# Last output-projection group in four column tiles of one PSUM bank, with the rest added by an identity product and two half copies

## Chip, cores, metric

One core of a Trainium2 chip. The metric is device time in microseconds (us) of one execution; lower is better. Before: 664.06 us, median of 3 runs (663.97 to 664.31).

## The reference, cut to what matters

```python
xn = layernorm(x)                                   # x: 4 x 1 x 640, bf16
q  = (xn @ wq) -> 4 x 32 heads x 128
p  = softmax(q @ k_cache^T * 128**-0.5)             # k_cache, v_cache: 4 x 32 x 4096 x 128
A  = (p @ v_cache -> 4 x 4096) @ wo                 # wo: 4096 x 640
out = x + A + gated_mlp(xn)                         # out: 4 x 640, bf16
```

Two caches of 134 MB each make nearly all of the 282.6 MB that the kernel moves. The heads are worked in four groups of eight. The last group's share of `@ wo`, and the adding up of all shares, is the last thing that happens. In the code below, PSUM is the memory that TensorE writes its sums to, a PSUM tile is a named piece of it (`ps_l.tile` and `misc_ps` allot one), and a bank is the block of PSUM in which the tile lies. In a profile line, 128\*4 or 64\*64 gives the rows and columns of a product's weights.

## The kernel before

The feed-forward part and the wo shares of groups 0 to 2 add up in one PSUM tile, `proj`: even wo pieces c in rows 0 to 63, odd ones in rows 64 to 127; within 64 rows, columns 0 to 319 of the output lie in rows 0 to 3, columns 320 to 639 in rows 32 to 35. VectorE adds those two halves and the residual `x_res` into `o_1`. The last group's pieces go to two further PSUM tiles, and VectorE adds those to `o_1`. The last group's wo is loaded in four parts: c = 0 to 3, 4 and 5, 6, 7.

```python
NG, HG, NH, NO2, B = 4, 8, 2, 320, 4
...
load_wo(NG - 1, (0, 4, 6, 7, 8))
...
o_1 = ppool.tile([64, NO2], F32)
nc.vector.tensor_tensor(out=o_1, in0=proj[0:64, 0:NO2], in1=x_res, op=ALU.add)
nc.vector.tensor_tensor(out=o_1, in0=proj[64:128, 0:NO2], in1=o_1, op=ALU.add)
last_a = ps_l.tile([64, NO2], F32)
last_b = misc_ps([P, NO2], F32)
last = [last_a, last_b[64:128]]
part = {1: 1, 3: 1, 5: 1}                # c = 1, 3, 5 to last_b, the others to last_a
for c in range(HG):
    p = part.get(c, 0)
    ...                                  # 32 columns of weights in a tile's first product, then 4
    for hf in range(NH):
        nc.tensor.matmul(last[p][32 * hf:32 * hf + nb, :], lhsT=lhsT,
                         rhs=wo_t[NG - 1][:, c, hf * NO2:(hf + 1) * NO2], start=..., stop=...)
    if c == 5:
        nc.vector.tensor_tensor(out=o_1, in0=last[1], in1=o_1, op=ALU.add)
o_bf = ppool.tile([64, NO2], BF16)
nc.vector.tensor_tensor(out=o_bf, in0=last[0], in1=o_1, op=ALU.add)
nc.sync.dma_start(out=out_flat[:, 0:NO2], in_=o_bf[0:B, :])
nc.scalar.dma_start(out=out_flat[:, NO2:NOUT], in_=o_bf[32:32 + B, :])
```

## Time and profile before

| | before |
|---|---|
| device time, median | 664.06 us |
| span of the profiled run | 662.5 us |
| DMA, mean | 427 GB/s |
| first product of the last group to store issue | 657.42 to 660.00 = 2.58 us |
| first c = 4 product to store issue | 658.21 to 660.00 = 1.79 us |
| clock of TensorE from 656.2 us on | 0.50 |

The kernel streams from HBM until about 658.5 us. Of the profile's rows only the last three can be touched by this change; the lines behind them are in the prediction. I call the stretch from the first product of the last group to the issue of the first store **the tail** in what follows. It starts with a landing load, so it can be compared between runs whose loads land at slightly different times.

### The profile page before, as it was taken

The numbers are of one execution on the slowest core, as the hardware profiler recorded it, in microseconds if no ns is written. First come the engines' busy times: TensorE is split into PE (matmuls) and PEld (weight loads), VectorE is DVE, ScalarE is ACT, GpSimd is POOL, SyncE is SP. The second block draws the span as 40 slices with busy tenths as digits, with TensorE's granted clock in tenths as the row PEclk, the third lists the DMA queues.
The fourth block names the chain that finished last, engine by engine and source line by source line (L and its number), as shares of the span: only waits on it lengthen the run. The fifth ranks groups of instructions, "written<-read, shape, count | busy, mean of one in ns | idle before, by whom it ended". The sixth has DMA issues, their size and how long they took to land.

```text
span 662.5 us, 5421 instructions
## 1 busy us (share of the span) xinstructions
PE 292.9 (44%) x2297; PEld 106.5 (16%) x2297; DVE 360.1 (54%) x275; ACT 78.4 (12%) x162; POOL 20.3 (3%) x64
## 2 busy tenths in 40 slices
PE   0636666256072556225336054533506254623245
PEld 0111122112021122111112022111202112211122
DVE  2249899556191759618256286745619185951112
ACT  0300000530100000530200000071010000053200
POOL 6210000000000000000000000000000000000000
PEclk9858768678577587677859596756958759667767
DMA  9999999999999999999999999999999999999996
GB/s 371 463 424 427 426 444 437 435 436 416 443 432 423 439 418 442 433 439 440 423 420 435 432 421 452 433 424 431 431 436 444 428 431 415 445 432 437 418 419 262
DMA packets 6901, 282.61 MB, mean 427 GB/s; under 512 B 808, under 2 KB 1084, under 8 KB 1468
## 3 DMA queue, kind: packets, MB, share of 16 engines
q1 hardware_dynamic: 6856, 282.25, 98.8%
q8 instruction: 18, 0.29, 0.2%
q14 instruction: 7, 0.06, 0.0%
q10 hardware_dynamic: 20, 0.01, 0.0%
HBM read 282.25 MB, written 0.01 MB: 426 GB/s over the span
## 4 chain that ended last, share of the span: by engine, by line
DMA 74%; DVE 11%; issue 11%; PE 2%; ACT 1%; SPq 0%; DVEq 0%; ACTq 0%
DMA kv<-in_A_k_cache_dram 64%; DVE kT L367 11%; DMA kv<-in_A_v_cache_dram 5%; DMA kv<-in_A_wo_dram 3%; DMA kv<-in_A_wq_dram 2%; PE O L449 2%; ACT xd L432 0%; ACT Zb L413 0%; ACT p L421 0%; DVE pT L425 0%; PE last_a L553 0%; DVE m L385 0%; PE S L378 0%; SPq L169 0%; PE misc L390 0%
## 5 line engine op out<-in xcount | busy, mean ns | idle before, releaser
L367 DVE STREAM_TRANSPOSE kT<-kv 128x2048 f32<-128x2048 f32 x128 | 282.8, 2276 | 124.7 <-DMA kv<-in_A_k_cache_dram 124.7
L378 PE MATMUL S<-kT,QZ 128*32 128x512 bf16 x1024 | 187.9, 500 | 230.6 <-DVE kT L367 230.6
L378 PEld LDWEIGHTS <-QZ 128*32 128x32 bf16 x1024 | 60.3, 111 | 353.4 <-issue 332.6
L449 PE MATMUL O<-kv,Zb 128*32 128x512 bf16 x1024 | 73.6, 451 | 58.2 <-DMA kv<-in_A_v_cache_dram 38.0
L458 DVE TENSOR_TENSOR om<-O,Mk 128x512 f32<-128x512 f32 x15 | 10.4, 692 | 109.0 <-PE O L449 109.0
L413 ACT ACTIVATE Zb<-xd,MkE 32x256 bf16<-32x256 bf16 x116 | 52.9, 498 | 110.4 <-PE O L449 109.0
L421 ACT ACTIVATE p<-S,negmax 128x512 bf16<-128x512 f32 x8 | 5.4, 683 | 400.6 <-DVE negmax L399 400.6
L449 PEld LDWEIGHTS <-Zb 128*32 128x32 bf16 x1024 | 32.9, 112 | 97.4 <-issue 55.8
L472 PE MATMUL misc<-R,SelR 128*32 128x128 f32 x32 | 6.4, 281 | 30.0 <-DVE R L459 28.4
L353 POOL COPY QZ<-qT 32x32 bf16<-32x32 bf16 x16 | 5.1, 318 | 390.6 <-PE S L378 389.9
L432 DVE COPY xd<-pT 32x256 bf16<-32x256 bf16 x44 | 16.0, 365 | 0.8
L459 DVE TENSOR_REDUCE R<-om 128x128 f32<-128x512 f32 x15 | 15.3, 1019 | 0.5
L432 ACT COPY xd<-pT 32x256 bf16<-32x256 bf16 x20 | 12.3, 614 | 5.6 <-DVE pT L425 5.2
L425 DVE STREAM_TRANSPOSE pT<-p 128x1024 bf16<-128x1024 bf16 x4 | 5.0, 1245 | 6.3 <-ACT p L421 6.3
L472 PEld LDWEIGHTS misc<-R,SelR 128*32 128x32 f32 x32 | 2.2, 107 | 37.8 <-DVE R L459 26.0
L385 DVE TENSOR_REDUCE m<-S 128x2 f32<-128x1024 f32 x4 | 4.9, 1225 | 5.5 <-PE S L378 5.5
L274 PE MATMUL q<-kv,xnT 128*32 128x512 bf16 x40 | 4.5, 630 | 6.9 <-DMA kv<-in_A_wq_dram 6.9
L461 DVE TENSOR_SCALAR R<-O,Mk 128x128 f32<-128x128 f32 x1 | 0.4, 351 | 12.5 <-PE O L449 12.5
L282 DVE CAST kv<-q 128x512 bf16<-128x512 f32 x1 | 0.7, 692 | 11.1 <-PE q L274 11.1
L390 PE MATMUL misc<-dg,ones_f 128*128 128x256 f32 x8 | 3.2, 488 | 7.6 <-DVE dg L387 7.6
L475 DVE SCALAR_TENSOR_TENSOR om<-misc,rinv,SelH 32x1024 bf16<-32x1024 f32 x4 | 5.1, 1271 | 2.0 <-PE misc L472 2.0
L437 PE MATMUL misc<-rowsum,SelPe 128*32 128x1 f32 x16 | 2.1, 202 | 9.0 <-ACT p L421 9.0
(102 smaller groups left out, 78.2 us busy)
## 6 DMA issues: line engine op xcount, KB each, us to landing
kv<-in_A_k_cache_dram SPq DMA_DIRECT2D x8, 4096.0 KB
kv<-in_A_v_cache_dram SPq DMA_DIRECT2D x1, 6144.0 KB
kv<-in_A_wq_dram SPq DMA_DIRECT2D x1, 5120.0 KB
kv<-in_A_wo_dram SPq DMA_DIRECT2D x3, 1280.0 KB
kv<-in_B_w_in_dram SPq DMA_DIRECT2D x1, 2160.0 KB, 19.9
kv<-in_A_v_cache_dram SPq DMA_DIRECT2D x1, 2048.0 KB
kv<-in_B_w_out_dram SPq DMA_DIRECT2D x1, 800.0 KB
kv<-in_A_wo_dram SPq DMA_DIRECT2D x1, 640.0 KB, 22.0
```

The costliest lines, as they stand in the source:

```text
L353: nc.gpsimd.tensor_copy(out=QZ[r0:r0 + 32, :, :, :, 8 + 8 * hp], in_=qT[32 * g:32 * g + 32, NE * hp:NE * hp + NE].rearrange("p e a b -> p ...
L367: nc.vector.transpose(kT[:].rearrange("p (t r) -> p t r", r=32), kw)
L378: nc.tensor.matmul(S_ps[32 * q:32 * q + 32, e], lhsT=QZ[:, b, 2 * kh + w, e, w0:w0 + 32], rhs=kb[:, i, :, e, :, w], start=(b == 0 and k < ...
L413: nc.scalar.activation(out=dst, in_=src, func=ACT.Copy, scale=mk)
L421: nc.scalar.activation(out=p_bf[:, :, e, :], in_=S_ps[:, e], func=ACT.Exp, bias=negmax[:, e:e + 1], scale=scale, accum_out=rowsum[:, e:e + 1])
L425: nc.vector.transpose(pT[:].rearrange("p t h x -> p (t h x)"), p_bf[:].rearrange("p t e m -> p (t e m)"))
L432: op(out=xd[32 * hp:32 * hp + 32, :, q, :], in_=pT[32 * q:32 * q + 32, :, hp, :].rearrange("p t x -> p x t"))
L449: nc.tensor.matmul(O_ps[32 * q:32 * q + 32, :, :], lhsT=Zb[b % 2][:, w].rearrange("p h c -> p (h c)"), rhs=vv[:, w * 4 * Dh:(w + 1) * 4 * ...
L458: nc.vector.tensor_tensor(out=om4[:], in0=O_ps[:], in1=Mk4[:, :, None].to_broadcast((P, 4, Dh)), op=ALU.mult)
L459: nc.vector.tensor_reduce(out=R, in_=om4[:].rearrange("p c d -> p d c"), axis=AX.X, op=ALU.add)
L472: nc.tensor.matmul(oh[:], lhsT=SelR[:, b].rearrange("p h b -> p (h b)"), rhs=state["R"][:, b, :], start=(b == 0), stop=(b == B - 1))
L475: nc.vector.scalar_tensor_tensor(out=om[:], in0=oh[:, None, :].to_broadcast((G, HG, Dh)), scalar=state.pop(("rinv", g))[:, 0:1], in1=MkH[: ...
```

## The change

It is meant to shorten what follows the last landing. All four column tiles of 32 take part for every c, so each product has 160 columns instead of 320. `o_1` no longer has to be added by VectorE: TensorE adds it with an identity matrix as weights (`ident_f`, in FP32). Two engines then copy half the result each.

```diff
-    last_a = ps_l.tile([64, NO2], F32)
-    last_b = misc_ps([P, NO2], F32)
-    last = [last_a, last_b[64:128]]
+    NQ = NO2 // 2
+    last = ps_l.tile([P, NQ], F32)
     ...
     for c in range(HG):
-        for hf in range(NH):
-            nc.tensor.matmul(last[p][32 * hf:32 * hf + nb, :], lhsT=lhsT,
-                             rhs=wo_t[NG - 1][:, c, hf * NO2:(hf + 1) * NO2], ...)
-        if c == 5:
-            nc.vector.tensor_tensor(out=o_1[:], in0=last[1], in1=o_1[:], op=ALU.add)
+        for k in range(2):
+            for hf in range(NH):
+                r0, n0 = 64 * k + 32 * hf, hf * NO2 + k * NQ
+                nc.tensor.matmul(last[r0:r0 + nb, :], lhsT=lhsT, rhs=wo_t[NG - 1][:, c, n0:n0 + NQ],
+                                 start=c == 0, stop=c == HG - 1)
+        if c == HG - 4:
+            for k in range(2):
+                nc.tensor.matmul(last[64 * k:64 * k + 64, :], lhsT=ident_f[:64, :64], rhs=o_1[:, k * NQ:(k + 1) * NQ],
+                                 start=False, stop=False)
-    nc.vector.tensor_tensor(out=o_bf[:], in0=last[0][:], in1=o_1[:], op=ALU.add)
+    nc.vector.tensor_copy(out=o_bf[:, 0:NQ], in_=last[0:64, :])
+    nc.scalar.copy(out=o_bf[:, NQ:NO2], in_=last[64:128, :])
```

(A padding column of zeros that the first products of the old layout needed, and its memset, go.)

More of the change, by code (lines that the diff above doesn't have):

```diff
@@ L484, in emit_oT @@
             nc.tensor.matmul(oT_ps[:, c, :], lhsT=om[:, c, :, :], rhs=B32[:], start=True, stop=True)
-        oT = small.tile([P, HG + 1, B], BF16, tag="oT", bufs=3)
-        nc.vector.tensor_copy(out=oT[:, 0:HG, :], in_=oT_ps[:])
-        if g == NG - 1:
-            nc.gpsimd.memset(oT[:, HG, :], 0.0)
+        oT = small.tile([P, HG, B], BF16, tag="oT", bufs=3)
+        nc.vector.tensor_copy(out=oT[:], in_=oT_ps[:])
         state[("oT", g)] = oT
@@ L540 @@
     nc.vector.tensor_tensor(out=o_1[:], in0=proj[64:128, 0:NO2], in1=o_1[:], op=ALU.add)
-    last_a = ps_l.tile([64, NO2], F32)
-    last_b = misc_ps([P, NO2], F32)
-    last = [last_a, last_b[64:128]]
+    NQ = NO2 // 2
+    last = ps_l.tile([P, NQ], F32)
     oT = state[("oT", NG - 1)]
-    part = {1: 1, 3: 1, 5: 1}
-    seen = set()
     for c in range(HG):
-        p = part.get(c, 0)
-        lhsT = oT[:, c, :] if p in seen else oT[:, c:c + HG, :].rearrange("p c b -> p (c b)")
-        nb = B if p in seen else 32
-        for hf in range(NH):
-            nc.tensor.matmul(last[p][32 * hf:32 * hf + nb, :], lhsT=lhsT,
-                             rhs=wo_t[NG - 1][:, c, hf * NO2:(hf + 1) * NO2], start=p not in seen, stop=c in (5, HG - 1))
-        seen.add(p)
-        if c == 5:
-            nc.vector.tensor_tensor(out=o_1[:], in0=last[1], in1=o_1[:], op=ALU.add)
+        lhsT = oT[:, c:c + HG, :].rearrange("p c b -> p (c b)") if c == 0 else oT[:, c, :]
+        nb = 32 if c == 0 else B
+        for k in range(2):
[7 more added lines that the diff above has]
+                                 start=False, stop=False)
     o_bf = ppool.tile([64, NO2], BF16, tag="p", name="o_bf")
-    nc.vector.tensor_tensor(out=o_bf[:], in0=last[0][:], in1=o_1[:], op=ALU.add)
+    nc.vector.tensor_copy(out=o_bf[:, 0:NQ], in_=last[0:64, :])
+    nc.scalar.copy(out=o_bf[:, NQ:NO2], in_=last[64:128, :])
     nc.sync.dma_start(out=out_flat[:, 0:NO2], in_=o_bf[0:B, :])
```

## The prediction

> **What bounds the kernel now.** I read the page's slice table first, then the chain of waits at the end, the timeline of the last microseconds, short windows over the same stretch, and the groups by line and shape for durations.
>
> The page says that the kernel streams: 427 GB/s in the mean, DMA at 90% or more in 39 slices of 40.
>
> ```profile
> DMA  9999999999999999999999999999999999999996
> DMA packets 6901, 282.61 MB, mean 427 GB/s; under 512 B 808, under 2 KB 1084, under 8 KB 1468
> ```
>
> The change touches nothing before the last loads of wo, so 656 us of the 662.5 us span cannot move. What it can move is the tail: from the last loads to the end. The timeline of that tail, before:
>
> ```profile
> 655.89 1.01 PE L496 MATMUL proj<-kv,oT 128*4 128x320 bf16 x16 [1.09 <-DMA kv<-in_A_wo_dram]
> 656.94 0.48 DVE L539 TENSOR_TENSOR o<-proj,x_res 64x320 f32<-64x320 f32 x1 [1.91 <-PE proj L496]
> 657.42 0.45 PE L553 MATMUL last_a<-kv,oT 128*32 128x320 bf16 x2 [0.52 <-DMA kv<-in_A_wo_dram]
> 657.46 0.49 DVE L540 TENSOR_TENSOR o<-proj,o 64x320 f32<-64x320 f32 x1
> ...
> 658.21 0.43 PE L553 MATMUL last_a<-kv,oT 128*4 128x320 bf16 x2
> 658.22 0.43 PE L553 MATMUL misc<-kv,oT 128*4 128x320 bf16 x2
> 658.62 0.83 PE L553 MATMUL last_a<-kv,oT 128*4 128x320 bf16 x4
> 658.62 0.08 PEld L553 LDWEIGHTS <-oT 128*4 128x4 bf16 x2 [0.32 <-issue]
> 658.70 0.49 DVE L557 TENSOR_TENSOR o<-misc,o 64x320 f32<-64x320 f32 x1 [0.74 <-PE misc L553]
> 659.02 0.08 PEld L553 LDWEIGHTS <-oT 128*4 128x4 bf16 x1 [0.32 <-issue]
> 659.49 0.48 DVE L560 TENSOR_TENSOR o_bf<-last_a,o 64x320 bf16<-64x320 f32 x1 [0.30 <-PE last_a L553]
> 660.00 0.30 SPq L561 DMA_DIRECT2D out_dram<-o_bf  x1
> 660.01 0.27 ACTq L562 DMA_DIRECT2D out_dram<-o_bf  x1
> ```
>
> The last group's wo comes in four pieces: columns c = 0 to 3 (0.66 MB), 4 and 5 (0.33 MB), 6 (0.16 MB), 7 (0.16 MB). Products start at 655.89 (the group before, 0.66 MB last), 657.42, 658.21, 658.62 and 659.02, so 1.53, 0.79, 0.41 and 0.40 us apart. Bytes over those gaps are 428, 415, 400 and 410 GB/s: the kernel's DMA rate. I therefore read each piece as starting when its load lands, also c = 6 and 7, where the page names "issue" because records of earlier products overlap. Then the end is: last landing 659.02, one product of 0.43 us, one VectorE add of 0.48 us, then store issue at 660.00 and 2.5 us to the end of the span.
>
> One more thing sets the sizes, the granted clock (columns: window, PE, PEld, DVE, ACT, POOL, clock, DMA share, GB/s):
>
> ```profile
> 652.80:656.20 3.40, 1.67 (x36) 1.17 (x39) 1.46 (x2) 0.00 (x0) 0.00 (x0) 1.00 0.85 341
> 656.20:659.60 3.40, 2.67 (x29) 0.74 (x20) 1.58 (x4) 0.00 (x0) 0.00 (x0) 0.50 0.24 84
> ```
>
> The tail runs at half clock. The same 320-column product takes 299 ns (median, L496) at full clock and 427 ns (L553) here: 133 + 166 and 267 + 160 with 320 columns at 2.4 and 1.2 per ns. So a product is its columns over the clock plus about 165 ns.
>
> **What the Trainium skill says.** (1) "TensorE: Matmul & The Clock Gate", section "What's actually happening": the array gets half its clock after an idle window of about 3.4 us, in free-running windows. The trace agrees: 1.00 to 0.50 at 656.2, and 2.4 and 1.2 columns per ns fit both durations. (2) "FP8 and Floating Point Precision", section "TensorE Precision Notes": true FP32 is four passes through the array. The trace agrees: each FP32 product has two records, and one of 256 columns takes at least 379 ns at full clock, which is 2 x 256 / 2.4 + 166. (3) "TensorEngine Tiling (Array Packing)", section "Key Properties": changing the tiling mode drains TensorE. The trace of before shows no such change with nothing else between, so this is untested. (4) "PSUM — Partial Sum Buffer", section "PSUM bank collisions raise a hardware error": two engines may use one bank at once if they are in different quadrants. So the two halves could be copied out side by side; whether the program lets them is another matter (below).
>
> **Removed.** Two 64x320 adds: the one at 658.70 (0.49 us) ends at 659.19 and is off the path; the final one (0.48 us at 659.49) is on it. The 320-column products become 160 columns wide, each c filling all four column tiles. For the last c that is 320 - 160 columns, 133 ns less at half clock (0.43 to 0.29 us). A GpSimd memset at 429 us goes, worth nothing.
>
> **Added 1: the identity products.** After c = 4 come two FP32 products of 64 rows, 64 weights and 160 columns. At half clock one record is two passes of 160: 2 x 160 / 1.2 = 267 ns of streaming, and there are four records, two per half. If the two halves ran fully side by side: 0.53 us. In order with the second record of one beside the first of the other: three steps, 0.80 us. Strictly one after another: 1.07 us. They also change the tile from 128x32 to 64x64 and back; if that drains the array, about 0.16 us each way (the fixed part of a product). Their input is ready in time: the second add ends at 657.95, and c = 4 lands at 658.21.
>
> Walk it with the middle choice and drains. c = 4 starts at 658.21, is through at 658.21 + 0.13 + 0.17 = 658.51. Identity streams to 659.31 and drains to 659.47. c = 5, 6 and 7, now all landed, take 3 x 0.133 us, and the last result is there at 659.47 + 0.40 + 0.16 = 660.03. Before it was 659.45: **plus 0.58 us**. Fully side by side and without drains: 658.35 + 0.53 + 0.40 + 0.16 = 659.44, no loss, no gain. Strictly in series with drains: plus 0.85 us. The slack between the landing of c = 4 and that of c = 7 is 0.81 us; c = 4 to 6 fill 0.40 us of it, so about 0.4 us of identity is free and the rest pushes the end.
>
> **Added 2: the two copies.** VectorE casts from PSUM: 128x32 in 192 ns and 128x512 in 692 ns, so 159 ns + 1.04 ns an element, and 64x160 is 0.33 us. ScalarE from PSUM: 320 elements in 437 ns and 512 in 586 ns, so 189 + 0.78 an element: 0.31 us. Side by side they would take 0.33 instead of 0.48 us, a gain of 0.15 us. But the listing of the built program's instruction order with the semaphores that each waits for shows the ScalarE copy waiting on VectorE's counter alone, not on TensorE's, and both stores waiting on ScalarE. VectorE's only late instruction is its own copy: the copies run **one after the other**. That is 0.33 + about 0.05 hand-over + 0.31 = 0.69 us for 0.48 us: **plus 0.21 us**.
>
> The sum of the middle case is +0.58 + 0.21 = +0.79 us. I take less than that as my point, because of the cases below.
>
> **Rivals.** *The change works as meant*: identity hidden in the load waits and copies side by side: -0.13 - 0.15 = -0.28 us, 663.8 us. For it: the input of the identity is early and 0.81 us of load time lies open. Against it: the half clock, and the semaphore listing, which is not an estimate. *Full clock in the tail*: windows run free, so unprofiled runs may meet the tail at full clock. Identity then streams in 0.40 us, c = 5 to 7 take 0.07 us each, and the walk ends at 658.21 + 0.23 + 0.40 + 0.17 + 0.20 + 0.16 = 659.37 against 659.02 + 0.30 = 659.32: plus 0.05, with the copies plus 0.26 us, 664.3 us. In the profiled run the clock fell exactly at 656.2, so this is the less likely one. *TensorE becomes the bound of the tail in full*: series and drains, +0.85 + 0.21 = +1.06 us, 665.1 us. *The copies alone count* (halves concurrent, no drains): +0.21 us, also 664.3 us. Nothing here reaches the loads: same sizes, same order, same waits.
>
> **Range and chances.** Weights by my reading: middle case 0.45 (664.85), copies alone or full clock 0.35 (664.3), series 0.15 (665.1), as meant 0.05 (663.8). The mean is 0.45 x 0.79 + 0.35 x 0.24 + 0.15 x 1.06 - 0.05 x 0.28 = +0.58 us, so 664.06 + 0.58 = 664.64; I say **664.6 us**. The runs of before spread over 0.34 us, a chip may differ as much, so the range is **664.1 to 665.2 us**. Two per cent is 13.3 us, more than the whole stretch from the landing of c = 4 to the end (4.3 us): within 2% at 0.99, faster and slower 0.005 each.
>
> **What would show it.** In the timeline after: c = 7's products no longer start at a fixed 0.40 us after c = 6's but follow it at 0.13 us, behind four FP32 records that span some 0.8 us (right), or c = 7 still starts near 659.0 with TensorE idle ahead of it (wrong: identity was hidden). The ScalarE copy starts after the VectorE copy's end and is released by it (right), or beside it (wrong). Copies of 0.33 and 0.31 us; store issue near 660.8 instead of 660.00. Loads landing at the same times, DMA near 427 GB/s. A time under 664.0 us would mean that the serial copies or the FP32 passes cost less than their shapes say; over 665.3 us, that the switch of tile mode costs far more than a drain.

## The result, and the profile after

The changed kernel took 664.62 us (median of 5; 664.49 to 665.95), the kernel before 664.31 us in all its 5 runs (663.97 to 665.42). The ratio is 1.0004, 95% interval 0.9992 to 1.0017. A ratio here is the mean time of one kernel's fast runs over that of the other's of the same rounds, so not quite the ratio of the medians quoted.

The interval is about 0.8 us either way, wider than the effect, because single runs of either kernel reach 665.4 and 665.9 us while most lie below 665. So single terms are read below from the traces, one for each version, and the medians are put beside them.

The timeline of the changed kernel's tail (start, duration, engine, line, operation; the idle time before it and its releaser in brackets):

```profile
657.48 1.09 PE L548 MATMUL last<-kv,oT 128*32 128x160 bf16 x20 [0.29 <-DMA kv<-in_A_wo_dram]
657.76 0.49 DVE L538 TENSOR_TENSOR o<-proj,o 64x320 f32<-64x320 f32 x1
658.27 0.09 PEld L548 LDWEIGHTS <-oT 128*4 128x4 bf16 x3 [0.30 <-issue]
658.50 0.80 PE L552 MATMUL last<-o,ident_f 64*64 64x160 f32 x4
659.23 0.57 PE L548 MATMUL last<-kv,oT 128*4 128x160 bf16 x12
659.85 0.32 DVE L556 CAST o_bf<-last 64x160 bf16<-64x160 f32 x1 [1.60 <-PE last L548]
660.20 0.29 ACT L557 CAST o_bf<-last 64x160 bf16<-64x160 f32 x1 [40.10 <-DVE o_bf L556]
660.52 0.30 SPq L558 DMA_DIRECT2D out_dram<-o_bf  x1
660.52 0.27 ACTq L559 DMA_DIRECT2D out_dram<-o_bf  x1
```

Two things are to be seen. First, c = 4 lands at 658.27 (the first weight load that had waited with it), the identity products run from 658.50, and the twelve products of c = 5, 6 and 7 follow in one block at 659.23, with no gap of 0.4 us between them any more: TensorE is late for c = 6 and 7, which have already landed (at 658.64 and 659.04 by the landing records). Their last result is there at 659.80, 1.53 us after c = 4's landing, where it was 659.45 - 658.21 = 1.24 us before: 0.29 us more. Second, ScalarE's copy names VectorE's as its releaser and starts when that has ended. From the last product to the store it is 0.72 us instead of 0.55: 0.17 us more.

The tail is 660.52 - 657.48 = 3.04 us instead of 2.58: **0.46 us more**. The span grew by 0.4, the median time by 0.31 us. From the store to the end of the span it is 2.41 us instead of 2.47, so 0.06 us of the tail's growth is given back there.

### The profile page after: what moved, and what is told of

Same layout as the page of the kernel before. It is cut to its first block, busy times and chain, and to the rows that moved or that the text cites. A ratio compares the mean times of both kernels' runs of the same rounds, so it can differ in the third digit from the quotient of the medians.

```text
span 662.9 us, 5457 instructions
## 1 busy us (share of the span) xinstructions
PE 292.8 (44%) x2317; PEld 106.8 (16%) x2317; DVE 359.8 (54%) x274; ACT 78.7 (12%) x163; POOL 20.2 (3%) x63
## 4 chain that ended last, share of the span: by engine, by line
DMA 74%; DVE 12%; issue 10%; PE 2%; ACT 1%; SPq 0%; DVEq 0%; ACTq 0%
DMA kv<-in_A_k_cache_dram 64%; DVE kT L367 11%; DMA kv<-in_A_v_cache_dram 5%; DMA kv<-in_A_wo_dram 3%; DMA kv<-in_A_wq_dram 2%; PE O L449 2%; ACT xd L432 0%; PE S L378 0%; ACT Zb L413 0%; ACT p L421 0%; DVE pT L425 0%; DVE m L385 0%; PE misc L390 0%; PE last L548 0%; SPq L169 0%
```

## The experiments

All ten runs were compared with runs of the kernel before on the same chip. All gave right results except the one that was not meant to. In the table, tail is the stretch defined above, read from each run's timeline; the median of before is that of the same call.

| kernel | tail, us | tail against before | median, us | before, us | ratio (95% interval) |
|---|---|---|---|---|---|
| before | 2.58 | | | | |
| the change | 3.04 | +0.46 | 664.62 | 664.31 | 1.0004 (0.9992 to 1.0017) |
| e1_two_banks | 2.73 | +0.15 | 664.29 | 664.33 | 1.0002 (0.9990 to 1.0014) |
| e2_early | 2.97 | +0.39 | 664.67 | 664.33 | 1.0005 (0.9993 to 1.0017) |
| e3_both | 2.64 | +0.06 | 664.51 | 664.33 | 1.0002 (0.9990 to 1.0014) |
| e4_one_sum | 2.34 | -0.24 | 664.00 | 664.33 | 0.9997 (0.9984 to 1.0010) |
| e5_same_half (wrong result) | 3.57 | +0.99 | 665.11 | 664.25 | 1.0013 (0.9998 to 1.0028) |
| e6_same_mode | 2.75 | +0.17 | 664.27 | 664.25 | 1.0001 (0.9984 to 1.0018) |
| e7_warm_before | 2.45 | -0.13 | 663.96 | 664.25 | 0.9996 (0.9981 to 1.0011) |
| e8_warm_after | 2.57 | -0.01 | 664.04 | 664.25 | 0.9997 (0.9982 to 1.0012) |
| e9_one_sum_warm | 2.27 | -0.31 | 664.11 | 664.29 | 0.9997 (0.9982 to 1.0011) |
| e10_mode_banks | 2.45 | -0.13 | 664.14 | 664.29 | 0.9997 (0.9985 to 1.0009) |

**The theory:** the loss is two separate terms, TensorE's time for the identity beyond what the load waits hide, and the two copies in series. **The rivals:** the copies could not run side by side anyway; the identity was hidden and something else moved the end; the half clock alone made the loss.

### Two banks

```diff
-    last = ps_l.tile([P, NQ], F32)
+    last_a = ps_l.tile([64, NQ], F32)
+    last_b = misc_ps([P, NQ], F32)
+    last = [last_a, last_b[64:128]]
```

(The products and copies now name `last[0]` or `last[1]`.)

> Only the two halves of the last group's sum lie in two PSUM tiles in two banks instead of one; all else as in the changed kernel. Theory (the copies are in series only because both read one PSUM tile): the built program's ScalarE copy now waits for TensorE itself; both copies start within 0.05 us of each other, about 0.04 us after the last product, and the stores issue 0.36 to 0.40 us after the last product instead of 0.72 us: 0.3 us less, about 664.3 us where the changed kernel has 664.6. Rival (two engines reading PSUM at once slow each other, or the shared output tile keeps them apart): copies in series still, or 0.5 us each, and no gain.

```profile
659.21 0.34 PE L550 MATMUL last_a<-kv,oT 128*4 128x160 bf16 x2
659.21 0.34 PE L550 MATMUL misc<-kv,oT 128*4 128x160 bf16 x2
659.59 0.32 DVE L558 CAST o_bf<-last_a 64x160 bf16<-64x160 f32 x1 [1.57 <-PE misc L550]
659.63 0.29 ACT L559 CAST o_bf<-misc 64x160 bf16<-64x160 f32 x1 [39.66 <-PE misc L550]
659.97 0.29 SPq L560 DMA_DIRECT2D out_dram<-o_bf  x1
```

In this timeline both copies name TensorE as their releaser, start 0.04 us apart and take 0.32 and 0.29 us, as long as they did in series: no sign that reading two banks at once slows either. From the last product to the store it takes 0.42 us, where 0.36 to 0.40 was expected. The tail is 0.31 us shorter than the changed kernel's. So the series came from the shared PSUM tile or its bank, which this edit split together; no run tells the two apart. It did not come from the shared output tile, which stayed shared here.

### Identity one step earlier

```diff
-        if c == HG - 4:
+        if c == HG - 5:
```

> Only the place of the two identity products changes: after c = 3 instead of after c = 4. Their input (second add) was ready at 658.25 in the changed kernel's profile (657.95 in that of before), c = 4 lands at 658.27. Theory (TensorE's 0.73 us of identity plus c = 5 to 7 fill the time after c = 4's landing, so the end is set by TensorE's queue): moving it ahead helps only as far as its input is earlier than c = 4's landing: last product's end 0 to 0.35 us earlier than in the changed kernel, counted from the landing of c = 4. Rival (identity is hidden by the load waits): no change of the end at all, with c = 7 starting 0.8 us after c = 4's landing in both.

```profile
657.93 0.80 PE L552 MATMUL last<-o,ident_f 64*64 64x160 f32 x4
658.66 0.71 PE L548 MATMUL last<-kv,oT 128*4 128x160 bf16 x16
660.08 0.29 SPq L558 DMA_DIRECT2D out_dram<-o_bf  x1
```

The first identity record started at 657.93, and all of c = 4 to 7 followed at 658.66. The tail was 2.97 us, 0.07 less than the changed kernel's; counted from c = 4's landing, as the theory had it, 0.04 less, near the low end of what it allowed. What speaks against the rival is c = 7: its products started at 659.01, 1.18 us after c = 4 landed, not 0.8. The input was the limit: the second add ended at 657.38 + 0.49 = 657.87, and c = 4 had landed at 657.83. The earlier place gains no time before the landing, only the order of two pieces of work changes.

### Both

The two edits above together.

> Both of these: two banks and identity after c = 3. Theory: the gains add, 0.3 us from the copies and 0 to 0.35 us from the place: 664.0 to 664.3 us, at or below the kernel before (664.3 in the same rounds). Rival (one term alone made the loss): the same as the better of the two single edits.

The tail was 2.64 us: 0.40 us less than the changed kernel's, 0.09 us less than with two banks alone. The gains add in the trace, though the second is hardly above what the landings differ by. The median of 664.51 us does not show it (664.0 to 664.3 was expected), with two of its five runs at 665.24 and 665.72; its lowest run was 664.11, against 664.18 for two banks and 664.08 for before.

### One sum from the start

No separate `last` and no `o_1`: two PSUM tiles of 64 rows x 160 columns in two banks take the feed-forward part, all four groups and the residual.

```diff
-    proj = ps_j.tile([P, 512], F32)
+    proj_a = ps_j.tile([64, NQ], F32)
+    proj_b = ps_l.tile([P, NQ], F32)
+    proj = [proj_a, proj_b[64:128]]
     ...
+    for k in range(2):
+        nc.tensor.matmul(proj[k][:], lhsT=ident_bf[:64, :64], rhs=x_res[:, k * NQ:(k + 1) * NQ], start=False, stop=False)
     emit_proj(NG - 3)
     ...
+    emit_proj(NG - 1)                     # 4 products of 160 columns for each c, into proj[k]
-    (o_1, last, and their adds)
+    nc.vector.tensor_copy(out=o_bf[:, 0:NQ], in_=proj[0][:])
+    nc.scalar.copy(out=o_bf[:, NQ:NO2], in_=proj[1][:])
```

> A version without the FP32 identity: the feed-forward part, all four wo groups and the residual (one bf16 identity product, at an early place) are summed in two PSUM tiles of 64 rows x 160 columns in two banks from the start, so nothing but two 160-column copies follows the last product. Theory (the loss of the change is identity plus serial copies, nothing else): c = 7 starts when its load lands, about 0.8 us after c = 4's, its product takes 0.29 us at half clock, stores issue about 0.38 us later: 0.27 us less than before from the landing of c = 4 to the store issue, about 664.0 us where before has 664.3. Rival (thirty-two narrow products per group are slower to issue than sixteen wide ones and eat it): no gain on before.

```profile
659.44 0.30 PE L499 MATMUL proj_a<-kv,oT 128*4 128x160 bf16 x2
659.86 0.30 PE L499 MATMUL proj_a<-kv,oT 128*4 128x160 bf16 x2
660.25 0.29 PE L499 MATMUL proj_a<-kv,oT 128*4 128x160 bf16 x2
660.59 0.32 DVE L544 CAST o_bf<-proj_a 64x160 bf16<-64x160 f32 x1 [4.19 <-PE proj_b L499]
660.63 0.29 ACT L545 CAST o_bf<-proj_b 64x160 bf16<-64x160 f32 x1 [38.71 <-PE proj_b L499]
660.97 0.30 SPq L546 DMA_DIRECT2D out_dram<-o_bf  x1
```

(This profiled run had its loads about 1.2 us late throughout; the tail is counted from its own landing.) The products of c = 4, 6 and 7 start at 659.44, 659.86 and 660.25, again 0.42 and 0.39 us apart with 0.3 us of work each: TensorE waits for each load, which also bears out the reading of the gaps before. c = 7 to the store takes 0.72 us, before it took 0.98: 0.26 less, where 0.27 was expected. This is what the change was meant to do, reached without its identity.

### Both identity products into the same half

```diff
-                nc.tensor.matmul(last[64 * k:64 * k + 64, :], lhsT=ident_f[:64, :64], ...
+                nc.tensor.matmul(last[0:64, :], lhsT=ident_f[:64, :64], ...
```

> A wrong result on purpose: the second identity product is sent to the same 64 rows of the sum as the first; shapes, order and waits as in the changed kernel. In the changed kernel's trace the four FP32 records start at 658.50 (two) and 658.83 (two), and c = 5 follows 0.73 us after the first: so the two halves seem to have run side by side, where the prediction took 0.80 us of streaming for them. Theory (side by side, because they use different column tiles): in one tile the four records follow one another, four streams of 0.267 us, and c = 5 starts 1.2 to 1.35 us after the first record; the end is 0.5 us later. Rival (the records were staggered, and the recorded starts mislead; the 0.73 us is three steps of 0.267 without a drain): four steps instead of three, c = 5 starts about 1.0 us after the first.

```profile
658.24 1.33 PE L552 MATMUL last<-o,ident_f 64*64 64x160 f32 x4
659.49 0.23 PEld L548 LDWEIGHTS <-oT 128*4 128x4 bf16 x12 [0.44 <-issue]
```

From the first FP32 record to c = 5 it took 1.25 us instead of 0.73, inside what the theory said and well above the rival's 1.0. Four records in one tile started at 658.24, 658.56, 658.82 and 659.09; in the changed kernel two started at 658.50 and two at 658.83. So in the changed kernel the two halves, of two records each, ran fully side by side. The tail grew by 0.53 us, and the median stands 0.86 us above before, where the change stood 0.31 above.

### Identity in tiles of 128 x 32

Rows 64 to 127 of `o_1` are zeros, set early by GpSimd.

```diff
-                nc.tensor.matmul(last[64 * k:64 * k + 64, :], lhsT=ident_f[:64, :64], rhs=o_1[:, k * NQ:(k + 1) * NQ],
-                                 start=False, stop=False)
+                for hf in range(NH):
+                    nc.tensor.matmul(last[64 * k + 32 * hf:64 * k + 32 * hf + 32, :], lhsT=ident_f[:, 32 * hf:32 * hf + 32],
+                                     rhs=o_1[:, k * NQ:(k + 1) * NQ], start=False, stop=False)
```

> The identity as four products of all 128 rows (the lower 64 of the second operand are zero) by 32 columns, one in each column tile, the shape of tile that the other products use, so that TensorE never changes its tiling. Result right. In the changed kernel, streaming explains 0.53 of the 0.73 us from the first FP32 record to c = 5, and c = 4 to the first record takes 0.23 us for a 0.13 us stream. Theory (the remaining 0.1 and 0.2 us are drains for the change of tile): c = 4 to identity about 0.14 us, identity to c = 5 0.55 to 0.60 us, 0.2 to 0.3 us less in all. Rival (the rest is the loading of FP32 weights, 0.29 us for four loads): eight loads instead of four, no less and perhaps 0.1 to 0.3 us more.

```profile
658.15 0.09 PEld L549 LDWEIGHTS <-oT 128*4 128x4 bf16 x3 [0.31 <-issue]
658.24 0.75 PE L554 MATMUL last<-o,ident_f 128*32 128x160 f32 x8
658.77 0.62 PE L549 MATMUL last<-kv,oT 128*4 128x160 bf16 x12
```

c = 4 to identity took 0.09 us instead of 0.23, identity to c = 5 0.53 instead of 0.73: 0.34 us less from c = 4 to c = 5, although there were eight records instead of four. The 0.53 us is two streams of 0.267 us and nothing else. So the rest of the identity's time in the changed kernel went with the change of tile shape. This edit changes two shapes at once (rows and columns of the tile), so which of them costs it is not separated, nor a drain from a slower weight load for the 64-wide tile (0.20 us against 0.15 us, median of one).

### The clock, in both kernels

```diff
+    busy_ps = ps_s.tile([P, HG * Dh], F32, tag="S", name="busy")
     emit_sel(NG - 1)
+    nc.tensor.matmul(busy_ps[0:32, 0:384], lhsT=SelR[:, 0], rhs=state["R"][:, 1:4, :], start=True, stop=True)
     emit_proj(NG - 2, range(0, 4))
     emit_oT(NG - 1)
+    for i in range(4):
+        nc.tensor.matmul(busy_ps[0:32, 0:512], lhsT=oT[:, 0:8, :], rhs=Zb[1][:, 0:16], start=True, stop=True)
```

(Shortened: a helper is written out, and the reshaping of the operands is cut. The products write to a tile that nobody reads.)

> The kernel before, with TensorE kept busy by products nobody reads (one FP32 of 384 columns after the last selection, four bf16 of 512 columns into a free bank after the last transposition), in gaps where it waits for loads. Theory (the half clock of the tail comes from the idle 650 to 656 us, and each product at the end pays for it): clock 1.0 through 659 us, the last product 0.30 instead of 0.43 us, 0.13 us less from the last landing to the store issue. Rival (the window that decides falls elsewhere): clock 0.5 in the tail as before, no gain.

> The changed kernel with the same busy products. Theory (half clock doubles what the identity costs): at clock 1.0 identity streams 0.27 us for two halves side by side, c = 7 is then on time for its landing 0.8 us after c = 4's or nearly so, and from c = 4's landing to the store issue it takes 0.81 + 0.23 + 0.04 + 0.67 = 1.75 us against 2.25 in the changed kernel and about 1.66 in the warmed kernel before: the loss shrinks from 0.46 to about 0.1 us. Rival (drains and weight loads, not streaming, make the identity's cost): 0.3 us or more of loss remains.

The windows of the warmed kernel before (columns as in the prediction):

```profile
652.80:656.20 3.40, 2.94 (x46) 1.64 (x39) 1.31 (x2) 0.00 (x0) 0.00 (x0) 1.00 0.85 342
656.20:659.60 3.40, 1.66 (x25) 0.53 (x16) 1.87 (x4) 0.00 (x0) 0.00 (x0) 1.00 0.21 74
```

With TensorE busy for 2.94 of 3.40 us instead of 1.67, the clock stays at 1.00 through the tail. (The first line is the stretch that preceded half clock in the kernel before. The clock's steps fall at other times in each trace; in this one they bound 651.59 to 655.01 us with 2.34 us of products and 655.01 to 658.42 with 2.25.) Chance could therefore have set the clock of a tail, but all nine profiled runs without busy products, before and changed included, had half clock for the whole tail, and all three with them full clock. The kernel before gains 0.13 us of tail, as expected for one 320-column product. The changed kernel gains 0.47:

```profile
658.33 0.49 PE L562 MATMUL last<-o,ident_f 64*64 64x160 f32 x4
658.75 0.46 PE L558 MATMUL last<-kv,oT 128*4 128x160 bf16 x12
659.27 0.32 DVE L566 CAST o_bf<-last 64x160 bf16<-64x160 f32 x1 [1.15 <-PE last L558]
659.62 0.29 ACT L567 CAST o_bf<-last 64x160 bf16<-64x160 f32 x1 [38.69 <-DVE o_bf L566]
659.93 0.29 SPq L568 DMA_DIRECT2D out_dram<-o_bf  x1
```

Identity to c = 5 now takes 0.42 us, and c = 5 to 7 no longer pile up behind it: c = 7's products start at 658.97, 0.81 us after c = 4's and right after their load, which landed at 658.93. Of the 0.46 us of loss, 2.57 - 2.45 = 0.12 us are left, about what the copies in series cost (0.17) less what the narrower last product saves at full clock (0.07). So at full clock the identity is hidden, at half clock it is not.

The medians of both fell by more than the tail alone explains for the kernel before (0.29 us against 0.13). Its loads also landed 0.16 us earlier in the profiled run. The busy products need have no part in that: two kernels without them show the same gap between tail and median (e5 +0.99 and +0.86, e6 +0.17 and +0.02), and e5's loads landed 0.21 us earlier than in the trace of before. Where the rest of the gap comes from is open.

### Two combinations

The version with one sum, warmed:

> The one-sum version (no identity of FP32, two banks, two copies side by side) with the products that keep the clock up. Theory (the gains seen apart are apart in cause, so they add): last product 0.23 instead of 0.29 us, from c = 7's landing to the store issue 0.23 + 0.04 + 0.38 = 0.65 us against 0.98 before; 0.33 us less than before, about 663.9 us or a little below; not more, since the 160-column product has only 0.07 us to lose to the clock. Rival (gains overlap): same as the warmed kernel before.

The change with both faults mended (two banks, identity in tiles of 128 x 32):

> The change with both its faults mended and nothing else: identity as four 128-row by 32-column products (no change of tile), the sum's halves in two banks. Theory (the loss was tile change plus serial copies): both gains add, 0.3 and 0.3 us, from c = 4's landing to the store issue 2.25 - 0.60 = 1.65 us against 1.79 before, so 0.1 to 0.15 us faster than before: about 664.1 us where before has 664.25. Rival (one mend hides the other): no better than 1.95 us, level with before plus 0.15.

```profile
659.39 0.29 PE L551 MATMUL last_a<-kv,oT 128*4 128x160 bf16 x2
660.66 0.32 DVE L560 CAST o_bf<-last_a 64x160 bf16<-64x160 f32 x1 [1.84 <-PE misc L551]
660.70 0.29 ACT L561 CAST o_bf<-misc 64x160 bf16<-64x160 f32 x1 [40.97 <-PE misc L551]
661.04 0.29 SPq L562 DMA_DIRECT2D out_dram<-o_bf  x1
```

The first took 0.66 us from the landing of c = 7 to the store (660.20 to 660.86; 0.65 expected). The second took 1.65 us from c = 4 to the store (659.39 to 661.04; 1.65 expected): the two mends add up in full, and the mended change is 0.13 us of tail faster than before, its order of work otherwise untouched. The shortest tail of all, 2.27 us, is that of the warmed one-sum version. Its median of 664.11 us (663.9 expected) is 0.18 below before, with an interval that holds 1.0; e4, e7 and e10 stand 0.15 to 0.33 us below before with the same reservation. No version is shown faster by these intervals; what is shown is a shorter tail, in one profiled run each. The nearest to a sign in the times is e5 to e8, where all four runs of each warmed kernel (663.87 to 664.13 us) lie below all seven of before (664.15 to 664.33).

## Why the prediction was right or wrong, point by point

The time of 664.62 us fell in the range, and beside the point of 664.6. The tail shows one term of the working mis-sized, the streaming of the identity's four records (0.80 us taken, 0.53 measured), and one case wrongly put together, halves side by side only without drains.

- **What bounds the kernel: right.** Every piece of wo is waited for. It was inferred from gaps that match the DMA rate; the one-sum version shows the same gaps of about 0.4 us around 0.3 us products.
- **Copies in series: right**, read from the order of semaphores before any run. Predicted +0.21 us, measured +0.17; the copies took 0.32 and 0.29 us for 0.33 and 0.31, and the hand-over 0.03 for 0.05. Two banks took it away.
- **Identity pushes the end: right in kind, too large in size.** Predicted +0.58 us to the last product, measured +0.29. The term at fault is the streaming of the four FP32 records: I took 0.80 us, three steps, assuming that the second record of one half runs beside the first of the other. They ran fully side by side, two steps, 0.53 us. The prediction had that case, but coupled it to "no drains" and so to no cost at all. With 0.53 us in its own walk and the drains kept, the last result comes 0.31 us later, near the 0.29 measured.
- **Drains: right in size, their nature not shown.** Twice 0.16 us were assumed; the switch of tile shape cost 0.34 us from c = 4 to c = 5, by a drain or otherwise. Without the switch (e6) the last result came 1.24 us after c = 4, as in the kernel before, and without any identity (e4) 1.12 us: on its own the identity costs 0.12 us, about what the narrower last product saves. What is left of e6's loss, 0.17 us, is that of the copies.
- **The half clock: right, and decisive.** With it removed, the loss goes from 0.46 to 0.12 us of tail. The rival "full clock" had put it at +0.26 us, because it used the staggered 0.40 us of streaming here too; with 0.27 us its walk gives about +0.14. That an idle window brought the half clock is less sure than the prediction has it: the stretch before it held 1.67 us of recorded products (see the last list).
- **Rival "as meant" (-0.28 us): wrong for this kernel**, yet the one-sum version's tail of -0.24 us shows that the intent itself was sound.
- **The point** was right partly by luck: middle case +0.79, weighted to +0.58; the traces say +0.46 and the medians +0.31 us. And the kernel before took 664.31 us in the rounds of the result where the prediction counted from 664.06: that shift of 0.25 us made up for most of what the forecast change was too large.

## What to carry to other kernels

An addition moved from VectorE to an idle TensorE is not free when it sits between the last load and the end: count its passes (FP32 here two records, each of two passes: 0.267 us for 160 columns at half clock), the clock that a waiting TensorE has at that moment, and the switch of tile shape, and keep the tile shape of its neighbours. Splitting a copy over two engines gains only if the build lets them start together: read each copy's semaphores, and give each engine its own PSUM tile in a bank of its own (as tried here, both at once). Better still, put what can be added early into the same accumulation from the start, so that nothing but a copy follows the last product.

## What the Trainium skill lacked or had wrong

- "TensorEngine Tiling (Array Packing)", section "Key Properties", says that a change of tiling mode drains TensorE, with no size. Here going to 64 x 64 tiles and back cost 0.34 us at half clock (c = 4 to c = 5 in 0.96 us, against 0.62 us with 128 x 32 tiles throughout); that it was a drain is not shown.
- The same page gives no time for FP32 products in several column tiles. At half clock two of them side by side took 0.73 us to the next product, in one tile one after the other 1.25 us; four in four column tiles took 0.53 us.
- "FP8 and Floating Point Precision", section "TensorE Precision Notes", gives four passes but not how a trace shows them: two records for each product, of 0.47 to 0.53 us each for 160 columns at half clock.
- "PSUM — Partial Sum Buffer", section "PSUM bank collisions raise a hardware error", allows two engines in different quadrants of one bank. The built program made them wait for one another all the same (ScalarE's copy released by VectorE's), with one PSUM tile in one bank; two tiles in two banks made the tail 0.31 us shorter. Whether the hardware would have allowed the one bank, no run here shows.
- "TensorE: Matmul & The Clock Gate", section "What's actually happening", ascribes half clock to an idle window of about 3.4 us without saying how idle. Here each stretch at one clock lasted a multiple of 3.41 us, and recorded busy time alone does not settle which comes next: after such a step with 1.78 us of products the clock fell to 0.50 (changed kernel, 652.20 to 655.61), after one with 1.77 us it stayed at 1.00 (e5, 650.21 to 653.63), and neither was idle.
